# A gated-attention, router and expert kernel: two weight-narrowing streams interleaved instead of run one after the other

## The chip, the cores and the metric

The kernel runs on one core of a Trainium2 chip. The metric is the device time of one execution in microseconds (us). PE is TensorE, DVE is VectorE, ACT is ScalarE, POOL is GpSimd, SP is SyncE, which issues most DMAs here.

## The reference

Three layers follow each other. The inputs w_in and w_out of the last one are stored as 64-bit floats.

```python
# gated linear attention, 4 x 8 heads, 768 steps, head size 48
f = 1/(1+exp(-f_logit))
state = f[t][:,None]*state + outer(k[t], v[t]);  y[t] = q[t] @ state
# a router: 3072 tokens to 8 experts of 384 tokens, by descending logit
logits = x @ w_gate;  ...;  out[mask_e] = relu(x[mask_e] @ w1[e]) @ w2[e]
# a common layer
h = x @ w_in;  out = (h*clip(h+3,0,6)/6) @ w_out      # 384 -> 2048 -> 384
```

## The kernel before, in words

The program has two stages. **Attention** goes over 24 chunks of 128 tokens, in the loop over j of `attention` (j is the chunk; two chunks make a unit u, whose decays, keys and queries are prepared one unit ahead). **Routing and experts** follow: a search for the experts' members, then 8 experts, each 128 x 384 matmuls on PE without much of a gap.

Each engine works through its instructions in the order in which the program text issues them (the schedule is manual), so that order is the plan. In a chunk it is: four slots `tg(0)` to `tg(3)`, between them the chunk's matmuls (`l_mm`: logits and output of the chunk before; `ya_mm`, `y_mm`, `kv_mm`: scores, outputs, new state), and the copies out of PSUM on ACT. A slot issues the DVE work of the next unit that is listed for it in `OPS` (scans L99 and L107, products L126), then what is `late`: the state update (L219 or L221 on DVE, then L222 on POOL) and the logits reduction L230. `a_ev` is the copy of the scores by ACT (L178) and their mask by POOL (L179), needed by `y_mm`. The state product L222 is needed by the next chunk's `ya_mm`.

Into the slots goes other work as filler: the generator `prep`, one `next` a step. It narrows the 64-bit weights to pairs of 32-bit floats (high and low part), which the common layer needs after attention:

- `prep_in`: w_in in 12 pieces of 128 x 512. A piece is fetched by a 512 KB DMA into "pw" (ring of 2, L948), joined by three DVE instructions into "pm" (ring of 2; L938, L940, L942 in `join`), one to a step, and split by `split_raw`: an ACT cast (L733) and a POOL subtraction (L734). The fetch of piece i+2 is issued behind the last join instruction of piece i.
- `prep_out`: the first 8 of 16 pieces of w_out, 128 x 384, in four steps each: 384 KB fetched three pieces ahead into a tile of its own (L967), three join instructions (L938, L940, L942) into "pm", an ACT cast (L973) and a DVE subtraction (L978). The other 8 follow behind attention, in tiles that lie where attention's pools were.

`both` (L1027) runs the second behind the first. `take` says how many steps a slot takes: PREP has 1, 0, 1 and 1 for the four slots of a chunk up to j = 20, and 2 in every slot behind that, until nothing is left.

```python
PREP=((1,0,1,1),(1,0,1,1)); END=(0,0)
```

Of the kernel before, what the change touches and what calls it, by code (L numbers as in the profile page):

```python
# [10 lines left out]
F32=mybir.dt.float32; F32R=mybir.dt.float32r; BF=mybir.dt.bfloat16; I32=mybir.dt.int32; U32=mybir.dt.uint32  # L11
# [6 lines left out]
def attention(tc, q,k,v,f,wg, x_dram, lg, ident, pmin, ranges, prep, setup, spin):  # L18
    nc=tc.nc
    ctx=ExitStack()  # L20
    with ctx:
# [35 lines left out]
        for s in range(2):  # L57
            for o in range(2):
                b=(s^o)*D
                nc.gpsimd.tensor_copy(SW[64*s:64*s+48,o::2,b:b+D],ident[64*s:64*s+48,None,64*s:64*s+D].to_broadcast([48,NP//2,D]))  # L60
        raw={}
        def load(u,nm,h0=0,h1=H):
            b,o=divmod(u*U,S)
            if nm!='v':
                src={'f':f,'k':k,'q':q}[nm]
                t=ld.tile([128,H,2*D],F32,name=nm+"r",bufs=2) if h0==0 else raw[nm,u]
                nc.sync.dma_start(t[:,h0:h1],bass.AP(tensor=src.tensor,offset=src.offset+b*H*S*D+h0*S*D+o*D,ap=[[2*D,128],[S*D,h1-h0],[1,2*D]]))
            else:
                t=VP[u%2]
                for c in range(2):  # L70
                    nc.sync.dma_start(t[:,c,:,:D],bass.AP(tensor=v.tensor,offset=v.offset+b*H*S*D+(o+c*C)*D,ap=[[D,C],[S*D,H],[1,D]]))
            raw[nm,u]=t
# [29 lines left out]
        def kept(u):  # L102
            PC[u]=pmin[:,u]
            nc.scalar.copy(PC[u],PX[u][:,:,:,G])
# [25 lines left out]
        def slot(u,n,fill=None):  # L130

            if u<NU and n in PET: PET[n](u)
            for f,*a in OPS.get(n,()) if u<NU else ():
                f(u,*a)
                if fill: fill(); fill=None
            while late: late.pop(0)()
            if fill: fill()
# [16 lines left out]
        def ya_mm(j):  # L154

            S=s_mm(j) if 0<=j<NCH and j%6 else None
            A=a_mm(j+1) if j+1<NCH else None
            if not S or not A:
                for p in range(NP):
                    for h in range(2):  # L160
                        for s in range(2):
                            if A: A(p,s,h)
                if S:
                    for p in range(NP):
                        for s in range(2): S(p,s)
                return
            for i,p in enumerate((0,2,1,3,None,None)):
                for s in range(2):
                    if p is not None: S(p,s)
                for s in range(2):  # L170
                    if i<2 or i>3: A(i if i<2 else i-2,s,1-s)
                for s in range(2):
                    if i>1: A(i-2,s,s)
        def a_ev(j,s):
            if s==0:
                AM[j]=wk.tile([128,2,NP,C],F32,name="am")
            am=AM[j][:,s]
            nc.scalar.copy(am,pA[j][s])  # L178
            nc.gpsimd.affine_select(out=am,in_=am,pattern=[[0,NP],[1,C]],compare_op=OP.is_ge,fill=0.0,base=0,channel_multiplier=-1)  # L179
# [10 lines left out]
        def y_mm(j,part):  # L190

            u,c=divmod(j,2); first=j%6==0
            vr=raw['v',u]; last=j==NCH-1
            rows=[slice(64*s,64*s+64) for s in range(2)]
            if part==0:
                if last: PY[j]=[ps.tile([128,NP,C],F32,name=f"pA{i}") for i in range(2)]
                else: PY[j]=[ps.tile([128,NP,C],F32,name="pT",bufs=PB) for _ in range(1 if first else 2)]*(2 if first else 1)
                return
            yt=wk.tile([128,NP,C],F32,name="yt")
            for p in (0,2,1,3):  # L200
                py=PY[j][p%2]
                for s in range(2):
                    nc.tensor.matmul(py[rows[s^p%2],p],vr[:,c,2*p+s],AM[j][:,s,p],start=first,stop=first or p>1)
                if p>1 and not first: nc.scalar.copy(yt[:,p%2::2],py[:,p%2::2])
            if first: nc.scalar.copy(yt,py)
            YT[j]=yt
# [17 lines left out]
        def l_mm(j):  # L224
            W=2*D+8
            px=ps.tile([128,512],F32,name="pT",bufs=PB)[:,:NP*W].rearrange("p (a e) -> p a e",a=NP)
            for p in (0,2,1,3):
                nc.tensor.matmul(px[:,p],YT[j][:,p],SW[:,p],start=True,stop=True)
            y=wk.tile([128,NP,2*D],F32,name="y")
            def logits(): nc.vector.tensor_reduce(lg[:,j],px[:,:,2*D:].rearrange("p a e -> p e a"),axis=AX.X,op=OP.add)  # L230
            if j==NCH-1: logits()
            else: late.append(logits)
            nc.scalar.copy(y,px[:,:,:2*D])
            later.append(lambda: nc.sync.dma_start(x_dram[j*C:(j+1)*C,:],y.rearrange("p a d -> p (a d)")))
# [37 lines left out]
        def refill(u,nm,i):  # L272
            if u<NU:
                {'f':decay,'k':keys,'q':queries}[nm](u,i)
                if u+1<NU and i==(0 if nm=='f' else 1): later.append(lambda: load(u+1,nm))
# [7 lines left out]
        PREP=((1,0,1,1),(1,0,1,1)); END=(0,0)  # L283
        for j in range(-1,NCH+1):
            tu,ti=divmod(j+1,2)
            tu+=1
            if j>=0 and j%2==0 and j//2+1<NU: load(j//2+1,'v')
            def take(i):
                for _ in range(PREP[ti][i] if j<21 else 2): next(prep,None)
            def tg(i): slot(tu,4*ti+i,(lambda: take(i)) if j>=0 else None)  # L290
            if j==NCH: spin(lambda: ps.tile([128,384],F32,name="pT",bufs=PB),TAIL[0])
            tg(0)
            if 0<=j-1<NCH: l_mm(j-1)
            if j==NCH: spin(lambda: ps.tile([128,384],F32,name="pT",bufs=PB),TAIL[1])
            tg(1)
            while later: later.pop(0)()
            if 0<=j<NCH: y_mm(j,0)
            ya_mm(j)
            if j+1<NCH:
                a_ev(j+1,0)  # L300
                a_ev(j+1,1)
            if ti==1: refill(tu+1,'f',2)
            if 0<=j<NCH: y_mm(j,1)
            if j>=0: kv_mm(j)
            tg(2)
            if ti==0 and tu<NU: kept(tu)
            if ti==0: refill(tu+1,'f',0)
            if j+1<NCH: kt_mm(j+1)
            if ti==1:
                for i in range(2): refill(tu+1,'q',i)  # L310
            tg(3)
            if ti==0: refill(tu+1,'f',1)
            if ti==1:
                for i in range(2): refill(tu+1,'k',i)
            if j>=0: next(constants,None)
            if j>=NCH-4: next(ranges,None)
            if j in (17,22,24): next(early)
            if j<20:
                for _ in range(END[ti] if j>=0 else 0): next(prep,None)
# [55 lines left out]
class Routing:  # L375
# [67 lines left out]
    def spin(s,tile,n):  # L443

        if not n: return
        t=tile()
        for _ in range(n): s.tc.nc.tensor.matmul(t[:,:128],s.ones,s.before,start=True,stop=True)
# [282 lines left out]
DM=384; F1=1024; F2=2048  # L730

def split_raw(nc, raw, hi, lo, eng_lo):
    nc.scalar.copy(hi, raw)  # L733
    eng_lo.tensor_tensor(out=lo, in0=raw, in1=hi.bitcast(F32), op=OP.subtract)  # L734
# [189 lines left out]
def gla_moe_ffn(tc,q,k,v,f_logit,moe_w_gate,moe_w1,moe_w2,moe2_w_in,moe2_w_out,out):  # L924
    nc=tc.nc
    with ExitStack() as ctx:
# [35 lines left out]
        def prep_out(pool,wr,g0,g1,ahead,W=DM):  # L962

            words={}
            for g in range(g0,g1): words[g]=wr.tile([128,DM,2],U32,name=f"wo{g}")
            def fetch(g):
                if g<g1: nc.sync.dma_start(words[g].rearrange("p c t -> p (c t)"),moe2_w_out[g*128:(g+1)*128,:].bitcast(U32))  # L967
            for g in range(g0,g0+ahead): fetch(g)
            yield
            done=None  # L970
            for g in range(g0,g1+1):
                yield
                if done: nc.scalar.copy(woh[g-1],done)  # L973
                if g<g1:
                    m=pool.tile([128,W],F32,name="pm",bufs=2)[:,:DM]
                    parts=join(m,words[g]); next(parts)
                yield
                if done: nc.vector.tensor_tensor(out=wol[g-1],in0=done,in1=woh[g-1].bitcast(F32),op=OP.subtract)  # L978
                if g==g1: return
                yield  # L980
                next(parts)
                yield
                next(parts,None)
                fetch(g+ahead)
                w=wr.tile([128,2,DM],F32R,name=f"wo{g}")
                woh[g],wol[g]=w[:,0],w[:,1]
                done=m
# [24 lines left out]
        def guarded(pool):  # L1012

            V=nc.vector
            for i in range(28):
# [8 lines left out]
                V.scalar_tensor_tensor(u,w[:,:,1],0xC0000000,u,op0=OP.bitwise_and,op1=OP.bitwise_or)  # L1024
                V.scalar_tensor_tensor(u,w[:,:,0],29,u,op0=OP.logical_shift_right,op1=OP.bitwise_or)
                split_raw(nc,m,hi,lo,V)
        def both(*gens):  # L1027
            for g in gens: yield from g
        def ranges(pt,bank):

            V=nc.vector
# [133 lines left out]
```

## Time and profile before

| | us |
|---|---|
| median of 3 runs (825.19 to 828.03) | 827.3 |
| profiled execution | 823.3 |
| its span, first to last instruction | 821.6 |
| busy: PE | 788.6 (96%) |
| busy: DVE | 547.6 (67%) |
| busy: ACT | 365.2 (44%) |
| busy: POOL | 125.1 (15%) |

Busy time is an average over stages that differ: in the experts, from about 180 us on, PE has nearly all of the span, and DVE's share falls. The profiled execution is 4.0 us below the median of the runs.

### The profile page before, as it was taken

Reading aid. Unit: us, or ns where it says so; the run is one execution under the profiler, and the core shown is the slowest. Engines: PE = TensorE matmul, PEld = TensorE weight load, DVE = VectorE, ACT = ScalarE, POOL = GpSimd, SP = SyncE. Lnnn points to the kernel's source line nnn. Section 1 sums busy time; section 2 is a strip of 40 time slices with the busy share of each in tenths; the row PEclk is TensorE's granted clock in tenths of the full one; section 3 lists DMA queues with packets and bytes.
Section 4 is the critical chain, followed back from the end, with each engine's and each line's share of the span. In section 5 each row is a group of like instructions: output and inputs, shape, how many; then the busy total and the mean of one; then the engine's idle time right before and its main releaser. Section 6 shows DMA issues by size and latency. Waiting matters only on the chain.

```text
span 821.6 us, 16654 instructions
## 1 busy us (share of the span) xinstructions
PE 788.6 (96%) x6385; PEld 757.5 (92%) x6385; DVE 547.6 (67%) x1517; ACT 365.2 (44%) x757; POOL 125.1 (15%) x215
## 2 busy tenths in 40 slices
PE   7999899879999999999999999999999999999994
PEld 7878798769999999899999999999999999999994
DVE  6999999777797468648856866587756524642431
ACT  6767776242445144415531642254235424541431
POOL 2656442120011001101010001100300020010001
PEclk9999999979999999999999999999999999999997
DMA  9999994550033013203322332322313332331000
GB/s 224 236 257 249 279 243 107 172 196 1 1 101 111 2 39 109 84 24 124 105 74 72 95 93 74 90 87 84 95 60 97 90 101 70 97 97 39 1 1 34
DMA packets 99033, 84.55 MB, mean 103 GB/s; under 512 B 67328, under 2 KB 86912, under 8 KB 98944
## 3 DMA queue, kind: packets, MB, share of 16 engines
q1 hardware_dynamic: 95872, 73.96, 32.0%
q0 software_dynamic: 3072, 9.44, 3.6%
q8 instruction: 52, 0.85, 0.4%
q14 instruction: 37, 0.30, 0.1%
HBM read 73.94 MB, written 9.44 MB: 101 GB/s over the span
## 4 chain that ended last, share of the span: by engine, by line
PE 62%; issue 9%; DVE 5%; DMA 2%; ACT 1%; POOL 1%; SPq 0%; POOLq 0%; DVEq 0%; ACTq 0%
PE pF L737 10%; PE acc L737 10%; PE acc L738 10%; PE pF L739 10%; PE pF L738 10%; PE acc L739 10%; DVE ga L882 1%; DVE hl L885 1%; PE pF L824 1%; POOL out_dram L916 1%; ACT hh L884 1%; DMA wo<-in_moe_w_out_dram 1%; DVE w1l L786 1%; DMA xg<-x_dram,q_ids 0%; PE pR L527 0%
## 5 line engine op out<-in xcount | busy, mean ns | idle before, releaser
L882 DVE SCALAR_TENSOR_TENSOR ga<-ga,pF 128x384 f32<-128x384 f32 x128 | 70.7, 553 | 99.9 <-ACT ga L880 99.5
L737 PE MATMUL acc<-wo,hh 128*128 128x384 f32 x384 | 132.9, 346 | 1.0 <-ACT hh L884 1.0
L737 PE MATMUL pF<-xh,wih 128*128 128x384 f32 x384 | 131.6, 343 | 0.0
L738 PE MATMUL acc<-wo,hl 128*128 128x384 f32 x384 | 129.6, 337 | 0.4 <-DVE hl L885 0.2
L738 PE MATMUL pF<-xh,wil 128*128 128x384 f32 x384 | 129.4, 337 | 0.0
L739 PE MATMUL acc<-wo,hh 128*128 128x384 f32 x384 | 129.3, 337 | 0.0
L739 PE MATMUL pF<-xl,wih 128*128 128x384 f32 x384 | 129.3, 337 | 0.0
L880 ACT ACTIVATE ga<-pF,three 128x384 f32<-128x384 f32 x128 | 74.3, 582 | 105.5 <-PE pF L739 101.1
L884 ACT CAST hh<-ga 128x384 fp32r<-128x384 f32 x128 | 65.7, 514 | 88.5 <-DVE ga L882 86.0
L845 ACT ACTIVATE hh<-pF 128x384 fp32r<-128x384 f32 x64 | 31.5, 492 | 131.8 <-PE pF L739 116.5
L916 POOL DMA_INDIRECT out_dram<-ga,q_ids x24 | 24.4, 1016 | 385.6 <-ACT ga L914 382.1
L885 DVE TENSOR_TENSOR hl<-ga,hh 128x384 fp32r<-128x384 f32 x128 | 71.0, 555 | 13.3 <-ACT hh L884 9.8
L846 DVE SCALAR_TENSOR_TENSOR hl<-pF,hh 128x384 fp32r<-128x384 f32 x64 | 35.5, 555 | 65.5 <-ACT hh L845 65.1
L737 PEld LDWEIGHTS acc<-wo,hh 128*128 128x128 f32 x384 | 72.1, 188 | 2.2 <-ACT hh L884 1.3
L738 PEld LDWEIGHTS acc<-wo,hl 128*128 128x128 f32 x384 | 72.2, 188 | 1.8 <-DVE hl L885 1.8
L738 PEld LDWEIGHTS pF<-xh,wil 128*128 128x128 f32 x384 | 72.2, 188 | 0.0
L737 PEld LDWEIGHTS pF<-xh,wih 128*128 128x128 f32 x384 | 72.2, 188 | 0.0
L739 PEld LDWEIGHTS pF<-xl,wih 128*128 128x128 f32 x384 | 72.1, 188 | 0.0
L739 PEld LDWEIGHTS acc<-wo,hh 128*128 128x128 f32 x384 | 72.0, 188 | 0.0
L737 PE MATMUL pF<-xh,w1h 128*128 128x384 f32 x192 | 66.6, 347 | 0.6 <-ACT xh L815 0.6
L737 PE MATMUL acc<-hh,w2h 128*128 128x384 f32 x192 | 66.1, 344 | 0.0
L739 PE MATMUL pF<-xl,w1h 128*128 128x384 f32 x192 | 65.0, 338 | 0.0
(285 smaller groups left out, 1605.4 us busy)
## 6 DMA issues: line engine op xcount, KB each, us to landing
wst<-in_moe_w_dram SPq DMA_DIRECT2D x58, 192.0 KB, 2.4
wst<-in_moe_w_dram SPq DMA_DIRECT2D x42, 256.0 KB, 2.8
pw<-in_moe_w_in_dram SPq DMA_DIRECT2D x12, 512.0 KB, 6.2
wo<-in_moe_w_out_dram SPq DMA_DIRECT2D x16, 384.0 KB, 5.8
pm<-in_moe_w_out_dram SPq DMA_DIRECT2D x32, 192.0 KB, 2.5
pm<-in_moe_w_in_dram SPq DMA_DIRECT2D x30, 192.0 KB, 2.5
v<-in_v_dram SPq DMA_DIRECT2D x24, 192.0 KB, 5.0
x_dram<-y SPq DMA_DIRECT2D x24, 192.0 KB, 4.6
```

The costliest lines, as they stand in the source:

```text
L737: nc.tensor.matmul(out, ahi, bhi, start=start, stop=False)
L738: nc.tensor.matmul(out, alo, bhi, start=False, stop=False)
L739: nc.tensor.matmul(out, ahi, blo, start=False, stop=stop)
L786: nc.vector.tensor_tensor(out=lo,in0=got[i],in1=hi.bitcast(F32),op=OP.subtract)
L824: nc.tensor.transpose(p[:,h*128:(h+1)*128],s.xg[:,h,d*128:(d+1)*128],s.ident)
L845: nc.scalar.activation(hh,p,AF.Relu)
L846: s.defer(2,lambda: nc.vector.scalar_tensor_tensor(hl,p,0.0,hh.bitcast(F32),op0=OP.max,op1=OP.subtract))
L880: nc.scalar.activation(a,p,AF.Relu,bias=s.three[:,0:1])
L882: late(f,n1,lambda: nc.vector.scalar_tensor_tensor(g,a,6.0,p,op0=OP.min,op1=OP.mult))
L884: late(f,n2,lambda: nc.scalar.copy(gh,g))
L885: late(f,n3,lambda: nc.vector.tensor_tensor(out=gl,in0=g,in1=gh.bitcast(F32),op=OP.subtract))
L916: st=nc.gpsimd.indirect_dma_start(out=s.out,out_offset=bass.IndirectOffsetOnAxis(ap=ids[:,t:t+1],axis=0),in_=o,in_offset=None)
```

## The change

`both` takes the two generators by turns: 7 steps of w_in, then six times 4 steps of w_out and 3 of w_in, then the rest of w_out, then the rest of w_in. The products of w_out's join get a ring of their own, "pmo", in attention (behind attention the name stays "pm"). And in chunks with j%4 = 1 up to j = 20 the third slot takes no step.

```diff
-                for _ in range(PREP[ti][i] if j<21 else 2): next(prep,None)
+                for _ in range((PREP[ti][i] if j%4!=1 or i!=2 else 0) if j<21 else 2): next(prep,None)
...
-                    m=pool.tile([128,W],F32,name="pm",bufs=2)[:,:DM]
+                    m=pool.tile([128,W],F32,name="pm" if W==DM else "pmo",bufs=2)[:,:DM]
...
-        def both(*gens):
-            for g in gens: yield from g
+        def both(a,b):
+            runs=[(a,7)]+[(b,4),(a,3)]*6+[(b,40),(a,40)]
+            for g,n in runs:
+                for _ in range(n):
+                    if next(g,'end')=='end': break
+                    yield
```

In the rows of the order below, pm<-pw is a join instruction of w_in, pm<-wo or pmo<-wo one of w_out, L221 the state update, L230 the logits reduction; lines behind both are four higher after the change.

**DVE, chunk 2 and the start of chunk 3.** Before:

```order
L221 TENSOR_TENSOR St_115<-St_115,pT 128x4x48
L938 TENSOR_SCALAR pm<-pw 128x512
L86 TENSOR_TENSOR pmq<-qr,ft 128x8x48
L126 TENSOR_TENSOR kh_113<-pT,S 128x512
L940 SCALAR_TENSOR_TENSOR pm<-pw,pm 128x512
L82 TENSOR_TENSOR pmk<-kr,ft 128x8x48
L942 SCALAR_TENSOR_TENSOR pm<-pw,pm 128x512
L99 SCALAR_TENSOR_TENSOR P_108<-ff_119,pC 128x259
```

After:

```order
L221 TENSOR_TENSOR St_115<-St_115,pT 128x4x48
L86 TENSOR_TENSOR pmq<-qr,ft 128x8x48
L126 TENSOR_TENSOR kh_113<-pT,S 128x512
L82 TENSOR_TENSOR pmk<-kr,ft 128x8x48
L938 TENSOR_SCALAR pmo<-wo_582 128x384
L99 SCALAR_TENSOR_TENSOR P_108<-ff_119,pC 128x259
```

The two steps of chunk 2 have become one that issues the three fetches and one that issues nothing, and the first instruction on w_out now stands at the start of chunk 3 instead of in chunk 13.

**DVE, chunks 21 and 22.** Before:

```order
L978 TENSOR_TENSOR wo_2498<-pm,wo_2498 128x384
L230 TENSOR_REDUCE lg<-pT 128x8
L940 SCALAR_TENSOR_TENSOR pm<-wo_1633,pm 128x384
L942 SCALAR_TENSOR_TENSOR pm<-wo_1633,pm 128x384
L221 TENSOR_TENSOR St_117<-St_117,pT 128x4x48
L938 TENSOR_SCALAR pm<-wo_1634 128x384
L978 TENSOR_TENSOR wo_2523<-pm,wo_2523 128x384
L940 SCALAR_TENSOR_TENSOR pm<-wo_1634,pm 128x384
L942 SCALAR_TENSOR_TENSOR pm<-wo_1634,pm 128x384
L1043 TENSOR_REDUCE q_w<-pT 3x1
```

After (pieces 9, 10 and 11 of w_in, with the range step L1047 and L1048 and the second state update between them):

```order
L938 TENSOR_SCALAR pm<-pw 128x512
L940 SCALAR_TENSOR_TENSOR pm<-pw,pm 128x512
L942 SCALAR_TENSOR_TENSOR pm<-pw,pm 128x512
L1047 TENSOR_REDUCE q_w<-pT 3x1
L1048 TENSOR_SCALAR q_eo<-ident,q_w 3x3
L938 TENSOR_SCALAR pm<-pw 128x512
L940 SCALAR_TENSOR_TENSOR pm<-pw,pm 128x512
L230 TENSOR_REDUCE lg<-pT 128x8
L942 SCALAR_TENSOR_TENSOR pm<-pw,pm 128x512
L938 TENSOR_SCALAR pm<-pw 128x512
L221 TENSOR_TENSOR St_115<-St_115,pT 128x4x48
```

Chunks 21 and 22 now hold w_in instead of w_out, and the state update of chunk 22 stands behind the first instruction of the last piece.

**POOL, chunks 21 to 23.** Before:

```order
L179 AFFINE_SELECT am<-am 128x512 x2
L222 TENSOR_TENSOR St_115<-St_117,pmin 128x4x48
L179 AFFINE_SELECT am<-am 128x512 x2
L222 TENSOR_TENSOR St_117<-St_115,pmin 128x4x48
L748 MEMSET three 128x1
```

After:

```order
L734 TENSOR_TENSOR wil<-pm,wih 128x512
L179 AFFINE_SELECT am<-am 128x512 x2
L222 TENSOR_TENSOR St_115<-St_117,pmin 128x4x48
L734 TENSOR_TENSOR wil<-pm,wih 128x512 x3
L179 AFFINE_SELECT am<-am 128x512 x2
L222 TENSOR_TENSOR St_117<-St_115,pmin 128x4x48
L734 TENSOR_TENSOR wil<-pm,wih 128x512
```

Five subtractions of w_in have come to the end; three of them, of pieces 8, 9 and 10, stand ahead of the mask and the state product of the last chunks.

## Rows read from the trace of the kernel before

**Rows 1.** Stages: length, busy PE, PEld, DVE, ACT, POOL; clock, DMA share, GB/s

```profile
25.00:95.00 70.00, 63.92 (x1092) 56.33 (x1088) 67.94 (x133) 53.35 (x120) 44.18 (x66) 1.00 0.98 255
128.00:148.00 20.00, 19.68 (x379) 18.20 (x381) 18.52 (x47) 12.35 (x30) 6.36 (x10) 1.00 0.27 72
```

**Rows 2.** DVE's waits, 25 to 149 us: total, times, longest

```profile
DVE St L221 <- PE pT L214: 5.0, 9, 1.1
```

**Rows 3.** Timeline of DVE: start, length; logits reductions in chunks 2, 12, 13, 17

```profile
32.23 0.17 DVE L230 TENSOR_REDUCE lg<-pT 128x8 f32<-128x32 f32 x1
...
93.67 0.17 DVE L230 TENSOR_REDUCE lg<-pT 128x8 f32<-128x32 f32 x1
...
97.82 0.16 DVE L230 TENSOR_REDUCE lg<-pT 128x8 f32<-128x32 f32 x1
...
120.55 0.16 DVE L230 TENSOR_REDUCE lg<-pT 128x8 f32<-128x32 f32 x1
```

**Rows 4.** The tile pm, 15 to 152 us: ns shortest/median/longest, first and last start

```profile
L938 DVE TENSOR_SCALAR pm<-pw x12: 399/685/1227, 21.8 to 87.5; 128x512 uint32<-128x512 uint32 x12
L940 DVE SCALAR_TENSOR_TENSOR pm<-pw,pm x12: 672/725/1172, 23.4 to 90.0; 128x512 uint32<-128x512 uint32 x12
L942 DVE SCALAR_TENSOR_TENSOR pm<-pw,pm x12: 674/679/1115, 24.5 to 91.5; 128x512 uint32<-128x512 uint32 x12
L733 ACT CAST wih<-pm x12: 617/652/680, 26.9 to 92.6; 128x512 fp32r<-128x512 f32 x12
L734 POOL TENSOR_TENSOR wil<-pm,wih x12: 1270/1379/1598, 27.6 to 93.3; 128x512 fp32r<-128x512 f32 x12
L938 DVE TENSOR_SCALAR pm<-wo x8: 344/352/529, 96.7 to 144.5; 128x384 uint32<-128x384 uint32 x8
L940 DVE SCALAR_TENSOR_TENSOR pm<-wo,pm x8: 541/548/554, 100.8 to 145.8; 128x384 uint32<-128x384 uint32 x8
```

**Rows 5.** Timeline of DVE, chunk 2, and the first instruction on w_out

```profile
33.27 0.35 DVE L221 TENSOR_TENSOR St<-St,pT 128x192 f32<-128x192 f32 x1 [0.40 <-PE pT L214]
...
34.93 0.68 DVE L126 TENSOR_TENSOR kh<-pT,S 128x512 f32<-128x512 f32 x1
35.53 1.17 DVE L940 SCALAR_TENSOR_TENSOR pm<-pw,pm 128x512 uint32<-128x512 uint32 x1
...
96.72 0.37 DVE L938 TENSOR_SCALAR pm<-wo 128x384 uint32<-128x384 uint32 x1
```

**Rows 6.** Timeline of SP's DMA issues: start, length

```profile
31.36 1.38 SPq L948 DMA_DIRECT2D pw<-in_moe_w_in_dram x1
32.79 1.02 SPq L67 DMA_DIRECT2D fr<-in_f_logit_dram x1
...
91.74 1.43 SPq L967 DMA_DIRECT2D wo<-in_moe_w_out_dram x3
```

**Rows 7.** DMA issues from 155 us on, KB each, us to landing; tile pw, all

```profile
wst<-in_moe_w_dram SPq DMA_DIRECT2D x58, 192.0 KB, 2.4
wst<-in_moe_w_dram SPq DMA_DIRECT2D x42, 256.0 KB, 2.8
...
DMA to landing us min/median/max: 6.2/6.2/6.2
```

**Rows 8.** Timeline of DVE, chunks 21 and 22

```profile
142.14 0.55 DVE L978 TENSOR_TENSOR wo<-pm,wo 128x384 fp32r<-128x384 f32 x1
...
146.81 0.27 DVE L1043 TENSOR_REDUCE q_w<-pT 3x1 f32<-3x128 f32 x1
...
148.61 0.35 DVE L221 TENSOR_TENSOR St<-St,pT 128x192 f32<-128x192 f32 x1 [0.48 <-PE pT L214]
```

**Rows 9.** Timeline of POOL: the mask of chunk 23, the state product

```profile
148.38 1.22 POOL L179 TENSOR_SCALAR_AFFINE_SELECT am<-am 128x512 f32<-128x512 f32 x2 [2.96 <-ACT am L178]
149.57 0.51 POOL L222 TENSOR_TENSOR St<-St,pmin 128x192 f32<-128x192 f32 x1
```

**Rows 10.** Stages of one us, columns as in rows 1

```profile
163.00:164.00 1.00, 0.14 (x4) 0.14 (x4) 0.93 (x9) 0.00 (x0) 0.00 (x0) 1.00 1.03 409
164.00:165.00 1.00, 1.00 (x19) 1.00 (x17) 0.83 (x6) 0.00 (x0) 0.00 (x0) 0.82 0.84 327
```

## The prediction

> **What bounds the kernel now.** I read the stages first. From 25 to 95 us, while the pieces of w_in are narrowed, VectorE (DVE) is busy 67.94 of 70 us, more than any other engine, and the DMA engines have a busy share of 0.98; from 128 to 148 us it is TensorE (PE) that has almost no gap, 19.68 of 20 us, and the DMA share has fallen to 0.27 [rows 1]. The list of DVE's waits shows the same from the other side: in this stretch DVE waited for nothing but the state update's matmul, 5.0 us in nine waits, and never for a DMA [rows 2]. So in attention every DVE instruction is on the path until about chunk 17, and after that every gap of PE is. What comes after attention (routing, then the experts on PE) starts when the last chunk ends, so a microsecond there is a microsecond of the total.
>
> A chunk with three w_in steps takes 6.14 us: the logits reduction at 32.23 and the one at 93.67 lie ten chunks apart. A chunk with three w_out steps takes 5.68 us: 97.82 to 120.55, four chunks [rows 3].
>
> **Part 1: DVE work leaves the bound part.** Up to chunk 20 the old schedule takes 64 steps: all 12 pieces of w_in (36 DVE instructions) and of w_out 18 instructions and 5 of the last kind (L978). The new one takes five fewer, 59: of w_in 23 instructions, of w_out 24 and 7. So 13 instructions of w_in go and 8 of w_out come. Medians of w_in are 685, 725 and 679 ns; of w_out 352 and 548, its third and fourth being like its second [rows 4]. Successive DVE instructions overlap by some 0.08 us (L126 at 34.93 lasts 0.68, and the next begins at 35.53 [rows 5]; the other pairs look alike), so I count 0.61 and 0.42: 13 x 0.61 - 8 x 0.42 = 4.6 us. Five of the twelve POOL subtractions (L734, 1379 ns each) leave with them. Beside one of them a w_in instruction lasts up to 1172 ns where its shortest lasts 672, some 0.5 us more [rows 4]: 5 x 0.5 = 2.5 us. Together 7.1 us of DVE time.
>
> Not all of it shortens the chunks, as PE is close behind. The two kinds of chunk tell how much: their prep differs by 3 x (0.61 - 0.42) + 0.5 = 1.07 us and their length by 0.46, so between four tenths and all of it: 2.8 to 7.1 us. I take 5.2, nearer the upper end, because most of the change falls where DVE, not PE, is full. **-5.2 us.** The dropped third step is in this count; it only lets DVE reach the state update earlier, which has to wait for PE anyway.
>
> What the POOL contention costs can be weighed against a rule. The Trainium skill, page "SBUF — State Buffer", section "SBUF: two separate sides", says that VectorE and GpSimd hold their shared port pair as an exclusive lock for a whole instruction, and that the loser fully blocks. The trace shows some 0.5 us, not a whole 1.38. If each subtraction cost DVE its whole length, part 1 would hold 4.6 + 5 x 1.38 = 11.5 us instead of 7.1, and the same fraction of it 8.4; that is a rival below.
>
> **Part 2: the first w_out words are late.** The first three w_out fetches move from chunk 12 to chunk 2, and the instruction that needs the first of them (L938 on wo) stands behind one empty step. In chunk 12 SP issued the three at 91.74 [rows 6], and DVE used the first at 96.72 without idling [rows 5]: SP ran ahead of DVE there. In chunk 2 it does not: SP issued fr at 32.79 with a w_in fetch of 1.4 us ahead of it [rows 6], which goes; so fr goes at about 31.4, x_dram's store after it, and the w_out words at about 33.1. They need at most 5.0 us (91.74 to 96.72) and at least 2.8, a 256 KB transfer on quiet engines [rows 7]; the engines are full, but 5.0 includes slack; I take 4.0: landed at 37.1. DVE gets there at 34.6: the state update (33.27) comes some 0.5 earlier, since chunk 1 gave up a step of 0.61, and then the update's 0.3 and L86, L126 and L82 with about 0.5 each are all that stands before L938 [rows 5]. So DVE stalls 2.5 us (1 to 3.5), and everything of the recurrence is queued behind it. **+2.5 us.** Later w_out fetches are three pieces ahead and are not waited for.
>
> **Part 3: the tail.** Steps 60 to 73 (chunks 21 and 22) were two pieces of w_out whose words had landed; now they are four pieces of w_in, with a DMA each and POOL work. A fetch of piece i+2 can only start when piece i has been read, so in the tail, where steps come without other DVE work between, the transfer shows. Word by word, on the old clock: L978 begins at 142.14 at the latest [rows 8], the last instruction of piece 7 ends near 143.3, SP issues the fetch of piece 9. A w_in transfer took 6.2 us in the full stretch; on quiet engines 192 KB took 2.4 and 256 KB 2.8 [rows 7], which makes 512 KB about 4.0 at 0.4 us for 64 KB (an estimate; ends 2.8 and 6.2). Piece 9 lands at 147.3, its three instructions end at 149.4; two short ones of the range step follow (the first is 0.27 [rows 8]), 149.9; piece 10, fetched at 146.0, lands at 150.0; its three and a logits reduction end at 152.2. Then, because queues are in order, the ScalarE (ACT) cast (0.65) and the POOL subtraction (1.38) [rows 4] run before the mask of chunk 23 (1.22) and the state product (0.51) [rows 9]: 155.95. The old trace had that product at 149.57, done at 150.08 [rows 9]. PE's last recurrence waits for it: **+5.9 us** (4.7 with 2.8 for the transfer, 8.0 with 6.2). The other way, through piece 11 to the state update that the old trace has at 148.61 [rows 8], comes out about a microsecond shorter, so it does not add. The leftovers, piece 11's cast and subtraction and its release of the pool, end before the last store of x_dram, which moves by the same 5.9, and cost nothing; if that cover went, the eight w_out fetches behind it would be late by up to 1.4.
>
> The separate ring "pmo" moves no instruction and costs nothing by itself; it keeps one kind's product from waiting for the other's. Bytes are the same; three w_in fetches of 512 KB leave the full stretch.
>
> **Sum.** -5.2 + 2.5 + 5.9 = +3.2 us. The profiled execution took 823.3 (span 821.6), which would become 826.5; the median of the runs is 827.3, 4.0 above the profiled one, so I forecast 827.3 + 3.2 = **830.5 us**. A difference under 0.3% (2.5 us) can't be told from none here.
>
> **Rivals.** (1) Faster: the waits are covered and DVE's relief decides. For it: chunk 12, where the same three fetches were not waited for; DMA has 3 x 512 KB fewer in the full stretch; and in the old tail DVE itself waited 0.48 for PE [rows 8]. Against it: SP is later than DVE in chunk 2, and the fetch that begins only when a piece is read. It decides if the first words land by 34.6 and a tail piece within about 2 us; then -5.2 plus the tail's casts and subtractions ahead of chunk 23's mask, about 1.7: -3.5, 823.8 us. (2) Only the tail waits: -5.2 + 5.9 = +0.7, 828.0. (3) A whole subtraction blocks DVE: -8.4, +2.5, +5.9, and in the tail two instructions more held by 0.9 each, +1.8: together +1.8, 829.1. It is the rule of the page named in part 1; the row of 672 to 1172 ns speaks against it. (4) The clock falls: PE idles for about 4 us before the last recurrence. In the old trace the granted clock was 1.00 (2.4 GHz) in the microsecond from 163, in which PE was busy for 0.14, and 0.82 as the mean of the next, in which it fell to the level of 1.2 GHz [rows 10]. At half clock the last chunk's PE work (about 2.5 us on the path) costs up to 2.5 more: 833.0. (5) The change does nothing: excluded, the order of DVE, SP and POOL differs.
>
> **Chances.** Forecast 0.55, of which 0.10 falls within 0.3% if the stall and the transfers come near their lower ends. Rival 1: 0.20, of which 0.02 within. Rival 2: 0.09, within but for 0.02 faster. Rival 3: 0.11, within. Rival 4: 0.05, slower. So faster 0.20, within 0.30, slower 0.50. The range goes from rival 1 (824) to the forecast with both transfers near their upper ends or the clock low: 835.
>
> **What would show it.** Right: DVE idles 1 to 3.5 us before the first L938 on wo, near 34 us, released by a DMA; the chunks between are 5.3 to 5.8 us; from 143 us on DVE idles before L938 on pw for DMA, POOL has three L734 in a row before a mask, and PE has a gap of some 4 us before the last state product; the last logits reduction of attention comes 2 to 5 us later. Wrong: no DMA among DVE's releasers, or chunk 21 begins more than 6 us earlier than before, or the loss lies behind 180 us.

## The result, and the profile after

The changed kernel took 833.7 us (median of 6 runs, 831.6 to 836.1) beside 825.7 for the kernel before in the same series: 1.0095 times as long, 95% interval 1.0078 to 1.0112, so 8.0 us slower (6.4 to 9.2). The forecast was 830.5, 3.2 us slower, with 824 to 835 as its range.

| | before | after |
|---|---|---|
| profiled execution, us | 823.3 | 834.6 |
| its span, us | 821.6 | 832.9 |
| counts of the range step begin (chunk 20), L1036 / L1040 | 141.06 | 139.04 |
| last logits reduction of attention ends | 153.34 | 161.22 |
| from the one to the other ("the way" below) | 12.28 | 22.18 |
| mean granted clock over the span | 0.989 | 0.978 |

After the change, line numbers from L975 to L1026 stand as they were and those behind `both` are four higher. The two marks of the table in the kernel before, and PE's last recurrence there (timelines of DVE and PE: start, length, engine, line; in brackets the engine's idle time just before, and what ended it):

```profile
141.06 0.31 DVE L1036 TENSOR_REDUCE q_cnt<-lg 128x1 f32<-128x160 f32 x1
153.15 0.19 DVE L230 TENSOR_REDUCE lg<-pT 128x8 f32<-128x32 f32 x1 [0.91 <-PE pT L228]
150.19 0.67 PE L152 MATMUL pA<-qt,St 64*64 64x128 f32 x16
150.79 1.09 PE L203 MATMUL pA<-am,v 128*64 128x128 f32 x16
151.97 1.14 PE L228 MATMUL pT<-sw,yt 128*128 128x104 f32 x8
```

After, the timeline of DVE; the lines answer to [rows 5] (the first two) and to [rows 8] (the others):

```profile
34.00 0.54 DVE L82 TENSOR_TENSOR pmk<-kr,ft 128x384 f32<-128x384 f32 x1
38.13 0.36 DVE L938 TENSOR_SCALAR pmo<-wo 128x384 uint32<-128x384 uint32 x1 [3.60 <-DMA wo<-in_moe_w_out_dram]
...
139.04 0.31 DVE L1040 TENSOR_REDUCE q_cnt<-lg 128x1 f32<-128x160 f32 x1
140.31 0.69 DVE L942 SCALAR_TENSOR_TENSOR pm<-pw,pm 128x512 uint32<-128x512 uint32 x1
142.34 1.49 DVE L942 SCALAR_TENSOR_TENSOR pm<-pw,pm 128x512 uint32<-128x512 uint32 x1
145.10 0.58 DVE L938 TENSOR_SCALAR pm<-pw 128x512 uint32<-128x512 uint32 x1 [1.26 <-DMA pw<-in_moe_w_in_dram]
145.71 1.65 DVE L940 SCALAR_TENSOR_TENSOR pm<-pw,pm 128x512 uint32<-128x512 uint32 x1
148.89 1.74 DVE L940 SCALAR_TENSOR_TENSOR pm<-pw,pm 128x512 uint32<-128x512 uint32 x1
152.52 1.10 DVE L938 TENSOR_SCALAR pm<-pw 128x512 uint32<-128x512 uint32 x1 [1.17 <-DMA pw<-in_moe_w_in_dram]
161.03 0.19 DVE L230 TENSOR_REDUCE lg<-pT 128x8 f32<-128x32 f32 x1 [1.18 <-PE pT L228]
```

Attention reaches chunk 20 2.0 us earlier although DVE has stood still for 3.60 us at its first w_out instruction: counted without that stop it would have been 5.6 earlier. Then all of it is lost. The way from chunk 20 to the end takes 9.9 us more. The same stretch on ACT, POOL and PE (their timelines; those of POOL answer to [rows 9]):

```profile
151.38 0.62 ACT L733 CAST wih<-pm 128x512 fp32r<-128x512 f32 x1 [2.27 <-DVE pm L942]
151.91 1.06 ACT L178 COPY am<-pA 128x512 f32<-128x512 f32 x2
152.86 0.66 ACT L204 COPY yt<-pT 128x256 f32<-128x256 f32 x2
```

```profile
145.35 1.46 POOL L734 TENSOR_TENSOR wil<-pm,wih 128x512 fp32r<-128x512 f32 x1
148.81 1.26 POOL L734 TENSOR_TENSOR wil<-pm,wih 128x512 fp32r<-128x512 f32 x1 [2.00 <-ACT wih L733]
152.08 1.26 POOL L734 TENSOR_TENSOR wil<-pm,wih 128x512 fp32r<-128x512 f32 x1 [2.00 <-ACT wih L733]
153.29 1.86 POOL L179 TENSOR_SCALAR_AFFINE_SELECT am<-am 128x512 f32<-128x512 f32 x2
155.12 0.94 POOL L222 TENSOR_TENSOR St<-St,pmin 128x192 f32<-128x192 f32 x1
```

```profile
153.30 2.04 PE L228 MATMUL pT<-sw,yt 128*128 128x104 f32 x8 [4.34 <-ACT yt L204]
156.11 1.13 PE L152 MATMUL pA<-qt,St 64*64 64x128 f32 x16 [0.78 <-POOL St L222]
157.18 1.97 PE L203 MATMUL pA<-am,v 128*64 128x128 f32 x16
159.16 1.83 PE L228 MATMUL pT<-sw,yt 128*128 128x104 f32 x8
```

Read from the right to the left. The last state product ends at 156.06; before, it ended at 150.08 [rows 9]. That is 6.0 us later by the clock and 8.0 against the chunk-20 mark. It waits for the mask, the mask for a subtraction and for the copy of the scores (L178), and the copy stands behind a cast in ACT's queue that waits 2.27 us for DVE. DVE, at the head, waits for words of w_in (1.26 us; its second wait, 1.17, comes behind the piece that the cast waits for) and is slow: three of its instructions last 1.49 to 1.74 us that last 0.69 elsewhere. Each ends about 0.55 us after the POOL subtraction beside it ends (145.35 + 1.46 = 146.81, and L940 ends at 147.36; 150.07 and 150.63). And PE has stood idle for 4.34 us by then. Its clock (stages; columns as in [rows 1], the granted clock is third from the end):

```profile
150.00:152.00 2.00, 0.00 (x0) 0.00 (x0) 1.35 (x3) 0.62 (x2) 0.08 (x1) 0.62 0.72 267
152.00:154.00 2.00, 0.70 (x3) 0.70 (x4) 1.48 (x3) 1.52 (x5) 1.92 (x2) 0.50 0.03 8
158.00:160.00 2.00, 2.00 (x17) 1.67 (x14) 1.79 (x7) 0.74 (x2) 0.00 (x0) 0.50 0.07 25
```

At 0.50 (1.2 GHz) the last recurrence takes 1.13, 1.97 and 1.83 us where it took 0.67, 1.09 and 1.14. From the end of the state product to the end of attention 5.16 us pass, before 3.26: 1.9 more. So the sum at the end of attention is -5.6 + 3.6 + 8.0 + 1.9 = +7.9 us, which is what the medians differ by. The profiled pair differs by 3.4 more, all behind attention. In the 30 us that follow it the mean granted clock is 0.83 before and 0.72 after, and later the two agree (1.00, then 0.98 in the last 180 us); how much of the 3.4 this makes was not tried. From the end of attention to the end of the span the fourteen profiled executions of this study take between 668.3 and 673.2 us, so their marks and ways are read beside the totals.

### The profile page after: what moved, and what is told of

The parts are those of the page before. It is cut to its first block, busy times and chain, and to the rows that moved or that the text cites. A ratio compares the mean times of both kernels' runs of the same rounds, so it can differ in the third digit from the quotient of the medians.

```text
span 832.9 us, 16643 instructions
## 1 busy us (share of the span) xinstructions
PE 793.7 (95%) x6385; PEld 762.7 (92%) x6385; DVE 548.6 (66%) x1517; ACT 365.4 (44%) x757; POOL 125.5 (15%) x215
## 4 chain that ended last, share of the span: by engine, by line
PE 67%; DVE 14%; issue 10%; DMA 3%; ACT 2%; POOL 1%; SPq 0%; POOLq 0%; DVEq 0%; ACTq 0%
PE acc L737 10%; PE pF L737 10%; PE acc L738 9%; PE acc L739 9%; PE pF L738 9%; PE pF L739 9%; PE pT L228 2%; PE pT L203 1%; PE pA L146 1%; PE pT L113 1%; DMA wo<-in_moe_w_out_dram 1%; DVE P L99 1%; DVE ga L882 1%; DVE hl L885 1%; DVE pm L940 1%
```

## The experiments

Theory: four terms, the relief, the stop at the first w_out words, the tail, the clock. First rival: the turns or the dropped step themselves cost. In the kernels of the runs some lines are a few numbers higher again. In the table the mark is the start of the first count in chunk 20, the way goes from there to the end of attention's last logits reduction, and the ratio is that to the kernel before in the same series (the changed kernel's is 1.0095, from a series of its own).

| run | mark | way | median us | ratio, 95% interval |
|---|---|---|---|---|
| 1 dropped step alone | 137.22 | 15.03 | 823.7 | 0.9975 (0.9962 to 0.9987) |
| 2 turns alone | 138.40 | 17.95 | 830.0 | 1.0045 (1.0030 to 1.0060) |
| 3 first words early | 139.41 | 21.76 | 831.8 | 1.0070 (1.0053 to 1.0088) |
| 4 tail of w_out | 141.68 | 19.25 | 831.6 | 1.0069 (1.0056 to 1.0083) |
| 5 tail subtraction on DVE | 139.44 | 20.98 | 831.2 | 1.0061 (1.0038 to 1.0084) |
| 6 third buffer in the tail | 137.88 | 21.37 | 830.7 | 1.0060 (1.0040 to 1.0081) |
| 7 PE kept busy | 139.49 | 20.92 | 832.3 | 1.0083 (1.0057 to 1.0109) |
| 8 first words one by one | 135.47 | 21.36 | 830.5 | 1.0055 (1.0034 to 1.0075) |
| 9 tail casts later | 140.64 | 20.31 | 831.9 | 1.0070 (1.0055 to 1.0086) |
| 10 three turns | 142.53 | 15.03 | 831.4 | 1.0080 (1.0054 to 1.0106) |
| 11 run 1, casts later | 138.88 | 13.52 | 823.2 | 0.9967 (0.9955 to 0.9980) |
| 12 mends 5, 6, 8, 9 together | 136.00 | 18.89 | 825.3 | 1.0001 (0.9989 to 1.0012) |

Each run has one profile, and the mark scatters: the changed kernel and runs 5, 7 and 9, whose instructions are the same up to it, have it between 139.04 and 140.64, and run 6, which differs there by the third buffer and one earlier fetch, at 137.88.

**Runs 1 and 2: each half alone.** The edit is run 1's; run 2 is the changed kernel with this line as it was before.

```diff
-for _ in range(PREP[ti][i] if j<21 else 2): next(prep,None)
+for _ in range((PREP[ti][i] if j%4!=1 or i!=2 else 0) if j<21 else 2): next(prep,None)
```

> The kernel before with the dropped step alone. Theory (waits): three w_in steps of 0.61 us and two w_out steps of 0.42 leave chunks in which VectorE is full, 2.7 us, and five w_out steps of 0.42 to 0.5 come to the tail; the two almost cancel: ratio to before 1.000, within 1.5 us; the last logits reduction of attention within 1 us of 153.15. Rival (TensorE sets the chunk length already): the chunks give nothing and the tail grows by 2.1 us: 828. In neither does the dropped step explain the 8 us.

> The changed kernel with all three steps in every chunk again. Theory (waits): the wait for the first w_out words stays, 3.0 us instead of 3.6 as VectorE comes 0.6 later; chunks are 2.5 us longer in sum; 64 steps lie before chunk 21 and 9 in the tail, so one piece of w_in (three instructions, one of them held by the subtraction) less there: 4 us off the tail. Together 831.5 (830 to 833). Rival (the turns themselves cost, or the dropped step is what gains): 835 or more, as five steps come back to full chunks.

The dropped step alone makes the kernel faster by 2.1 us: the mark comes 3.8 us earlier and the way takes 2.8 more, so 1.1 of it is seen in the profile. That is more than "almost cancel", and neither theory nor rival foresaw it. The turns alone cost 3.7 us by the ratio, against 7.8 with the dropped step: with three steps in every chunk a piece less is left for the tail, whose way falls by 4.2, as expected. The chunks did not do as expected. The mark came 0.6 us earlier than in the changed kernel, where 1.9 later had been worked out (2.5 for the steps that come back, less 0.6 of the wait), and the wait for the first words was 1.9 us instead of 3.0. With the turns in place the dropped step gains nothing up to chunk 20 that stands out of the mark's scatter. So the dropped step is a gain where the tail is w_out and a loss where the tail is w_in.

**Runs 3 and 8: the first words.** In run 3 the three fetches go out three steps earlier; in run 8 one goes out then, and two more after each piece used.

```diff
-runs=[(a,7)]+[(b,4),(a,3)]*6+[(b,40),(a,40)]
+runs=[(a,4),(b,0),(a,3),(None,1),(b,3),(a,3)]+[(b,4),(a,3)]*5+[(b,40),(a,40)]
...
-for g in range(g0,g0+ahead): fetch(g)
+nxt=g0+(1 if W!=DM else ahead)
+for g in range(g0,nxt): fetch(g)
...
-fetch(g+ahead)
+for h in range(nxt,min(nxt+2,g+ahead+1)): fetch(h); nxt=h+1
```

Here (b,0) is a step of b without a turn of its own, and None an empty step, so that DVE's order stays; the lower two hunks are run 8's alone.

> The changed kernel with the first three w_out fetches issued three steps (one chunk) earlier and VectorE's order as it is. Theory (waits): VectorE does not wait at its first w_out instruction (3.6 us in the changed kernel), nor TensorE with it; the chunk-20 mark (L1040's instruction, 139.04 in the changed kernel) comes 3 to 3.6 us earlier; the tail is as it was: 830.3 (829.5 to 831.5), ratio to before 1.0045 to 1.007. Rival (the DMA engines are full, so the words only push others back): the next w_in piece or forget-gate load is waited for instead, and less than 1.2 us is won: 832.5 or more.

> The changed kernel with one w_out piece fetched at first, a chunk earlier, and two more with each piece used until three are ahead (the third run fetched all three early, and its wait moved to query and key loads). Theory (a burst of three pieces, 1.2 MB, is what the full DMA engines can't take): neither the wait of 3.6 us for w_out words nor waits for qr and kr of over 1 us in sum; the chunk-20 mark comes 2.5 to 3.6 us sooner than in the changed kernel (139.04), and the total is 830 to 831. Rival (any byte put ahead of others there is waited for): more than 2 us of DMA waits stay, chunk-20 mark within 1 us.

In run 3 the wait for w_out words went and others came. DVE's list of waits from 15 to 60 us:

```profile
DVE pmq L86 <- DMA qr<-in_q_dram: 2.2, 2, 1.3
DVE pmk L82 <- DMA kr<-in_k_dram: 1.5, 1, 1.5
```

That is 3.7 us in all, but not all of it is the words' doing. One of the waits for qr ended at 23.32, before the words were issued (24.34):

```profile
23.32 0.56 DVE L86 TENSOR_TENSOR pmq<-qr,ft 128x384 f32<-128x384 f32 x1 [1.34 <-DMA qr<-in_q_dram]
```

So 2.3 us of new waits took the place of 3.6. The mark did not move (139.41), as the rival said; the total, 831.8, lies between the theory's 830.3 and the rival's 832.5. In run 8 no w_out words are waited for at the first use, and the mark is at its theory's place:

```profile
135.47 0.31 DVE L1045 TENSOR_REDUCE q_cnt<-lg 128x1 f32<-128x160 f32 x1
```

3.6 us of stop, 3.57 us of mark; against the scatter of the mark the agreement is better than it could be counted on, but 135.47 is 2.4 below the lowest of the marks above. The wait of 1.4 us for qr that stayed ended at 22.77 and is again the one ahead of the words. So three pieces at once, 1.2 MB, in a stretch in which the DMA engines are full (share 0.98 [rows 1]) cost a stop of 3.6 us in one place and waits of 2.3 in another, whoever reads last, and one piece alone cost none.

**Run 4: w_in's rest before w_out's.**

```diff
-runs=[(a,7)]+[(b,4),(a,3)]*6+[(b,40),(a,40)]
+runs=[(a,7)]+[(b,4),(a,3)]*6+[(a,40),(b,40)]
```

> The changed kernel with what is left after the six turns taken in the other order, w_in first, so that the tail is w_out as in the kernel before. Theory (waits in the tail): of the relief in chunks 17 to 20 1.5 to 3.4 us is lost, the state product's delay of 8.0 against the chunk-20 mark falls to 1 or less, TensorE has no gap over 1 us before the last recurrence and its clock stays at 1.00 there: 826.5 (825 to 828.5), about the kernel before. The first w_out wait of 3.6 us stays. Rival (the turns, not the tail, cost the time): 831 or more.

A miss: 831.6 instead of 826.5, a total that the rival had named (831 or more). Its reason, that the turns themselves cost the time, does not follow: run 12 keeps the turns and loses nothing. The way fell by 2.9 us only, and the mark came 2.6 later. Pieces 7 to 10 of w_in now lie in chunks 17 to 20 and put a POOL subtraction ahead of a mask; PE's gap there grew (busy 0.92 of the 2 us from 122, 2.00 in the changed kernel) and was followed by half clock, as was the one in the tail (stages):

```profile
124.00:126.00 2.00, 0.71 (x5) 0.48 (x6) 2.00 (x5) 0.00 (x0) 0.39 (x1) 0.83 1.06 206
126.00:128.00 2.00, 2.00 (x10) 2.00 (x11) 2.00 (x5) 0.94 (x3) 0.00 (x0) 0.50 0.35 95
...
150.00:152.00 2.00, 1.89 (x36) 1.90 (x40) 1.32 (x5) 0.89 (x2) 0.05 (x1) 0.50 0.03 8
154.00:156.00 2.00, 2.00 (x26) 1.91 (x24) 0.20 (x1) 0.84 (x3) 0.94 (x2) 0.50 0.00 0
```

Piece 11 and two subtractions were still in the tail. "As in the kernel before" was wrong about that: there w_in had ended by chunk 12.

**Runs 5, 6, 7 and 9: the links of the tail, one each.** Run 5 puts the tail's subtractions on DVE, run 6 adds a buffer from piece 7 on, run 7 gives PE matmuls of its warm-up kind in the gap, run 9 issues the cast (and subtraction) one step later.

```diff
-split_raw(nc,m,wih[:,i//4,c],wil[:,i//4,c],nc.gpsimd)
+split_raw(nc,m,wih[:,i//4,c],wil[:,i//4,c],nc.vector if i>6 else nc.gpsimd)
```

```diff
-got[i]=pool.tile([128,512,2],U32,name="pw",bufs=2)
+got[i]=pool.tile([128,512,2],U32,name="pw",bufs=3)
...
-fetch(i+2)
+fetch(i+2 if i<7 else i+3)
+if i==6: fetch(9)
```

```diff
+if j==NCH-1: spin(lambda: ps.tile([128,384],F32,name="pT",bufs=PB),56)
 if 0<=j-1<NCH: l_mm(j-1)
```

```diff
-split()
+late=i>7
+if not late: split()
 m=pool.tile([128,512],F32,name="pm",bufs=2); c=slice(i%4*512,i%4*512+512)
-yield from join(m,got[i])
+parts=join(m,got[i]); next(parts)
+yield
+if late and 1==1: split()
+next(parts)
+yield
+if late and 1==2: split()
+next(parts,None)
```

Of the last edit's two lines with `late and`, the first applies and the second never does.

> The changed kernel with the subtractions of the five w_in pieces that end in the tail on VectorE instead of GpSimd. Theory (a GpSimd subtraction holds VectorE): VectorE's w_in instructions in the tail last 0.69 and 0.42 again instead of 1.49, 1.65, 1.74 and 1.10, some 3.9 us less, against five subtractions of 0.61 = 3.1 more; the mask of chunk 23 no longer stands behind a subtraction; the last state product comes 1 to 2 us sooner: 832.3. Rival (VectorE is not held, it has its work): 3 us more work, 835 to 836.5.

> The changed kernel with a third buffer for w_in's words, used from piece 7 on, so that the tail's pieces are fetched one piece earlier. Theory (transfers show in the tail): the two waits for w_in words, 1.26 and 1.17 us, go, the casts that follow them come earlier, and the last state product 2.4 us sooner: 831.3; 829.5 if TensorE's gap becomes too short for its clock to fall. Rival (the queues of ScalarE and GpSimd decide, the waits only fill slack): under 0.8 us, 833 or more.

> The changed kernel with 56 small matmuls (67 ns each, 3.8 us) on TensorE in its gap before the recurrence of chunk 22, nothing else. Theory (the clock costs 1.9 us of the tail): the granted clock stays at 1.00 from 148 to 161 us, L228's, L152's and L203's groups last 1.14, 0.67 and 1.09 instead of 2.04, 1.13 and 1.97, and the last logits reduction comes at 159.1 instead of 161.0: 831.8. Rival (the clock's fall is beside other work): last logits reduction within 0.5 us of 161.0, 833.5.

> The changed kernel with the ScalarE cast (and GpSimd subtraction) of the pieces in the tail issued one step later, so that the cast of piece 10 stands behind the score copies and the yt copies of the last chunk in ScalarE's queue and not ahead of them. Theory (in the tail ScalarE, waiting for VectorE's last w_in step, holds up attention's own copies): the score copy moves from 151.9 to about 149.5, TensorE's gap of 4.3 us before the recurrence of chunk 22 shrinks below 2, the state product comes 1.5 us sooner (then held by the wait for w_in's words), and the way from the chunk-20 mark to the last logits reduction falls from 22.0 to 18.5 us: 830.2. Rival (VectorE's amount of work sets the tail's length): under 1 us.

Run 5: no instruction on w_in lasts over 1.00 us, most 0.42 or 0.69, and with five instructions more on DVE the way is still 1.2 us shorter. DVE itself is hardly sooner: its last join instruction ends 16.4 us behind the mark, before 16.7, as it now waits 2.9 us for casts. The copy of the scores stays at 12.9 us behind the mark; what is gained is the mask, which starts 0.7 sooner against the mark, no longer behind a subtraction, and takes 1.43 us instead of 1.86. The gap on PE stayed (4.24 us), since the casts still stand ahead of attention's copies. Run 6: both waits for words are gone, but the state product came only 1.0 sooner against the mark (153.94 - 137.88 = 16.06, after 17.02), near the rival's bound. Only the first wait had been on its path: in the changed kernel the second holds up the state update (153.54), which is done 1.2 us before the product starts all the same. And DVE, now without waits, is held in other places (L938 for 1.47 us, L942 for 1.50 and 1.65). Run 7: the clock did not stay full as expected. It fell under the spins (0.60 in the 2 us from 152, 0.54 in those from 154), and they held PE until 155.98, but from 156 on it was full, and the last recurrence took what it took before the change (PE's timeline):

```profile
151.23 4.91 PE L448 MATMUL pT<-r_before,r_ones 128*128 128x128 bf16 x56 [1.82 <-DVE lg L230]
155.98 1.09 PE L228 MATMUL pT<-sw,yt 128*128 128x104 f32 x8
157.00 0.67 PE L152 MATMUL pA<-qt,St 64*64 64x128 f32 x16
157.60 1.09 PE L203 MATMUL pA<-am,v 128*64 128x128 f32 x16
158.78 1.14 PE L228 MATMUL pT<-sw,yt 128*128 128x104 f32 x8
```

1.3 us of the 1.9 came back in the way; in the totals the interval leaves it open. Run 9: the copy of the scores moved from 12.9 to 10.0 us behind the mark (150.62 - 140.64), as the theory said, and the state product from 17.0 to 15.0; the way from 22.2 to 20.3, half of what was expected, since PE then waited 2.54 us for the state product and the clock fell all the same:

```profile
150.62 1.08 ACT L178 COPY am<-pA 128x512 f32<-128x512 f32 x2
155.69 1.13 PE L152 MATMUL pA<-qt,St 64*64 64x128 f32 x16 [2.54 <-POOL St L222]
```

Each run thus freed one link, and the next took over part of it.

**Run 12: four mends together.** The edits of runs 6, 8 and 9, with the cast one step later and the subtraction, on DVE as in run 5, one step after it.

> The changed kernel with the mends of runs 5, 6, 8 and 9 together: first words one piece at a time, a third buffer for w_in's words from piece 7 on, and for the five pieces of the tail the cast one step later and the subtraction on VectorE one step after that. Alone, the three of the tail took 1.1, 1.0 and 1.9 us off the way from the chunk-20 mark to the last logits reduction (22.0 us; 12.1 in the kernel before), and run 8 brought the mark from 139.0 to 135.5. Theory (separate queues and waits that add): way of 18 us or less, last logits reduction by 153.5, total 825 to 827, about the kernel before. Rival (one chain, VectorE's work of four w_in pieces, sets the tail, and each mend only uncovers the next link): way of 20 us or more, total 829 or more.

825.3 beside 825.5: the whole loss is gone, with the turns and the dropped step kept. The mark is at 136.00, the way 18.89, a little longer than the theory's 18 (which is measured to the start of the last reduction, some 0.2 less), and the rival's 20 and 829 are excluded. A wait of 0.7 us for the second w_out piece is left, and attention still ends 1.55 us later than in the profile before. The count in chunk 20 and DVE's last reductions of attention:

```profile
136.00 0.31 DVE L1055 TENSOR_REDUCE q_cnt<-lg 128x1 f32<-128x160 f32 x1
154.61 0.28 DVE L230 TENSOR_REDUCE lg<-pT 128x8 f32<-128x32 f32 x2
```

**Runs 10 and 11: in search of a faster one.** Run 10 takes three longer turns; run 11 is run 1 with w_out's casts and subtractions a step later.

```diff
-runs=[(a,4),(b,0),(a,3),(None,1),(b,3),(a,3)]+[(b,4),(a,3)]*5+[(b,40),(a,40)]
+runs=[(a,4),(b,0),(a,3),(None,1),(b,3),(a,9)]+[(b,4),(a,9)]*2+[(a,40),(b,40)]
```

> Three turns instead of six (four w_out steps, nine w_in steps), then the rest of w_in, then w_out, so that w_in ends by chunk 17 and the tail is w_out; the first words fetched one piece at a time as in the eighth run; the dropped step stays. Theory: no early wait, chunk-20 mark at 136.3 (137.2 with the dropped step alone, 135.5 in the eighth run), a tail of 15.0 us as in the first run, last logits reduction at 151.3: 822.8 (821.5 to 824.5), ratio 0.9965. Rival (w_in near the end of attention puts gaps into TensorE, and its clock falls, as in the fourth run): last logits reduction after 154, 827 or more.

> The kernel before with the dropped step and with w_out's ScalarE cast and VectorE subtraction one step later each (the third join instruction before them). Theory (ScalarE's casts hold up attention's copies in the tail): the score copies of the last two chunks come 1 to 2 us sooner and the last logits reduction at 150.5 instead of 152.0: 822.0, ratio 0.995. Rival (VectorE's work sets it): as the first run, ratio 0.9975.

Run 10 missed by 8.6 us, and the rival's figures came (a last reduction after 154, 827 or more). Its way is 15.03, exactly run 1's with the same kind of tail; its mark is 6.2 later than expected. 3.0 of that is a wait for the second w_out piece, which the edit fetched one step ahead of its use:

```profile
DVE pmo L938 <- DMA wo<-in_moe_w_out_dram: 3.0, 1, 3.0
```

Run 8 fetches it one step ahead too, but there 5.2 us lay between the issue (44.83) and the use (50.07), here 1.1 (61.07, and DVE ready at 62.22). Beside run 8, 3.9 us more lie between the logits reductions of chunks 13 and 21. In that stretch a subtraction (124.31) stands ahead of a mask, PE is busy for 0.66 of the 2 us from 126, and the clock is 0.56 in the 2 us from 128 and 0.59 in those from 130, as the rival said; the rest was not taken apart. Run 11 has a way 1.5 us shorter than run 1 but a later mark. Its last reduction came at 152.12 and not at the theory's 150.5, and its total can't be told from run 1's, as its rival said. Both are faster than both kernels; the dropped step alone is the simpler.

## Why the prediction came out as it did

The direction and the range held, and the relief, the stop, the late pieces and PE's gap showed in their places. The size was 4.8 us short, in three terms; of the signs named, the last logits reduction came 7.9 us later and not 2 to 5. That 833.7 lies in the range is in part luck: its upper end of 835 was drawn from slow transfers or a low clock, and while the clock did fall, the transfers came within 0.3 us of their estimates; held instructions made up the difference.

- **Part 1, -5.2.** The size came out: 5.6, as mark plus stop in the changed kernel, and 5.6 again as the plain mark in run 8 (141.06 - 135.47). Mark plus stop in runs 5, 6, 7 and 9 gives 4.4 to 7.0, so rival 3's 8.4 was not met, but so close an agreement is in part luck. The composition is not confirmed. By the prediction's way of counting (0.61, 0.42 and 0.5 us, and 5.2 of 7.1 of the sum), the dropped step alone would be worth 1.5 us and the turns alone 2.7; the marks show 3.8 (run 1) and 4.6 (run 2, 2.7 of mark and 1.9 of stop), and the two do not add up. The half microsecond for a subtraction is right as a mean, but the row of 672 to 1172 ns does not speak against a block for a whole instruction. The L940 of 1.17 us at 35.53 [rows 5] began inside a subtraction and ended 0.54 us after it; the product beside it (L126, 34.93) kept its 0.68. In the kernel before, eight of the twelve subtractions lengthen DVE's instructions, against the shortest of their kind, by 0.69 to 0.84 us in sum and four by 0.06 at most, 0.55 in the mean. The four meet scans, products from PSUM and small instructions, which keep their length (L107 and L126 in the subtraction at 39.30), and joins that began before them. Timelines of POOL and DVE, before:

```profile
34.56 1.60 POOL L734 TENSOR_TENSOR wil<-pm,wih 128x512 fp32r<-128x512 f32 x1
39.30 1.49 POOL L734 TENSOR_TENSOR wil<-pm,wih 128x512 fp32r<-128x512 f32 x1 [0.34 <-ACT wih L733]
39.57 0.68 DVE L107 TENSOR_TENSOR_SCAN S<-ff,pC 128x259 f32<-128x259 f32 x1
40.64 0.68 DVE L126 TENSOR_TENSOR qt<-pT,P 128x512 f32<-128x512 f32 x1
```

- **Part 2, +2.5.** Mis-sized: 3.60. DVE came at 34.53, forecast 34.6. The failed step is SP's: it issued the words at 33.87, not 33.1. It came to fr sooner than forecast (30.81, not 31.4), but the issues of fr and of x_dram's store took until 33.87, 3.1 us where the forecast left 1.7; the transfer took 4.3 instead of 4.0 (SP's timeline, answering to [rows 6]):

```profile
30.81 1.61 SPq L67 DMA_DIRECT2D fr<-in_f_logit_dram  x1
32.51 1.31 SPq L234 DMA_DIRECT2D x_dram<-y  x1
33.87 1.60 SPq L967 DMA_DIRECT2D wo<-in_moe_w_out_dram  x3
```

- **Part 3, +5.9.** Mis-sized: 8.0 against the mark. The estimate of 4.0 for the transfer was good (fetched after 141.00, there at 145.10: 4.1). What failed is the step "its three instructions end" 2.1 us after the words: they took 3.0 for piece 9 and 2.9 for piece 10, one of each held until a subtraction's end; and the mask and product, beside DVE's work, took 1.86 and 0.94 instead of 1.22 and 0.51 [rows 9]. 0.9 + 0.7 + 0.6 + 0.4 = 2.6, less small gains. Rival 3's tail clause, two instructions held by 0.9 each, was right (0.96 and 1.05); I had put it in a rival that was tied to the chunks. The Trainium skill, page "SBUF — State Buffer", section "SBUF: two separate sides", has the loser of the port pair wait for the whole instruction, where VectorE's instruction has two SBUF inputs or runs in a 2-port mode. The trace agrees: the held joins end 0.55 us after the subtraction in the tail (L938 of piece 11 0.28), whenever they began, and 0.28 to 0.56 after it in the chunks before. It does not agree for the scans, which also read two tiles of SBUF (ff and pC) and kept their 0.68 us. What differs in the tail is that DVE has hardly anything but joins to run beside a subtraction.
- **The clock.** Given 0.05 as rival 4, it happened, at 1.9 of the 2.5 us worked out for it. Run 7 gave 1.3 of it back. The row it went by [rows 10] has the clock hold through a microsecond with PE at 0.14 and fall in the next one; the gap forecast here was four times as long, and the chance was too low.
- **"Leftovers cost nothing"**, and the ring "pmo" as well, were not tried by themselves. Nothing in the traces speaks against them.

Rival 1 (waits covered), rival 2 (only the tail waits) and rival 5 (no change) did not occur.

## What to carry to other kernels

Work that is spread over a pipeline's steps should run out in its cheapest and most local kind: here a tail of short instructions on landed data, none of them on POOL, takes 12 to 15 us from the mark (the kernel before, runs 1, 10 and 11), and one with a transfer, a cast and a subtraction for each piece 18 to 22. When an order is changed, follow each moved piece through every in-order queue it enters (SP, ACT, POOL), and ask which of the main chain's instructions stand behind it at the end, where no slack is left. And a first fetch of several pieces into full DMA engines was paid by whichever reader came last: fetch one, and each next one early enough (run 10 waited 3.0 us for its second).

## What was not expected of the hardware

The clock can fall in one execution and not in another behind what looks like the same gap. In the changed kernel and in run 9, whose instructions are in the same order up to chunk 20, PE's busy time agrees within 0.01 us from 124 to 128 us; the first kept the full clock, the second fell to 0.50 (stages of the changed kernel, then of run 9):

```profile
124.00:126.00 2.00, 0.74 (x8) 0.42 (x4) 2.00 (x4) 0.84 (x2) 0.65 (x2) 1.00 0.27 80
126.00:128.00 2.00, 1.70 (x14) 1.50 (x15) 2.00 (x7) 1.01 (x3) 0.00 (x0) 1.00 0.00 0
```

```profile
124.00:126.00 2.00, 0.75 (x8) 0.42 (x4) 2.00 (x4) 0.86 (x2) 0.67 (x2) 1.00 0.38 118
126.00:128.00 2.00, 1.69 (x11) 1.48 (x11) 2.00 (x7) 0.99 (x3) 0.00 (x0) 0.81 0.00 1
128.00:130.00 2.00, 2.00 (x19) 1.82 (x22) 2.00 (x5) 1.44 (x5) 0.00 (x0) 0.50 0.00 0
```

Run 9's mark, 1.6 us later than the changed kernel's, is read with that in mind. What decides it stays open.
